# Weight conversions subtracted by TensorE in PSUM, and a head that copies the first grams' blocks first, in a kernel of attention and two expert layers

## Chip, cores and metric

The kernel runs on one core of a Trainium2 chip, in one launch. The metric is the device time of one execution in microseconds (us). TensorE (PE) multiplies matrices into PSUM; VectorE (DVE), ScalarE (ACT) and GpSimd (POOL) do the rest, each with a queue of its own that it works off in order.

## The reference

Three parts follow one another. The first is delta-rule attention over 4 batches, 8 heads, 768 tokens and 48 columns:

```python
k_n = k / (np.linalg.norm(k, axis=-1, keepdims=True) + 1e-06)
for t in range(S):
    y[:, :, t] = einsum('bhd,bhde->bhe', q[:, :, t], state)
    v_old = einsum('bhde,bhd->bhe', state, k_n[:, :, t])
    state = state + beta[:, :, t] * outer(k_n[:, :, t], v[:, :, t] - v_old)
```

The second works on its output as 3072 tokens of 384 columns: `h = x @ w_in` (384 to 2048 columns), `g = max(0.01 * h, h)`, `g @ w_out` (back to 384). The third picks one of eight experts for each token by the largest gate logit, computes `max(x @ w1[e], 0) @ w2[e]` and scales the row by the gate's probability and a sigmoid. The weights w_in and w_out come as 64-bit floats.

## The kernel before

The 768 tokens are cut into 12 chunks of 64. A chunk's attention is solved in closed form: a gram matrix of its keys (`gram`, line 104, TensorE, 48 or 64 wide tiles), its inverse by elimination (`inverse`, lines 207 to 211), and a chain of small matmuls that carries the state on (`chain`). Every operand of TensorE is two fp16 halves, high and low, and a product is three passes (high by high, high by low, low by high). The low half is the remainder: the source less the high half.

Chunks are handled in pairs w = 0 to 5. `k_load` brings the keys (kt), `k_split` makes the halves kc, `q_split` the halves q, `k_gram` multiplies and `k_gram_out` copies out of the gram's banks: the diagonal blocks go to td (eight small copies a chunk, line 131), the others as halves to lx (ScalarE the high half, line 141, VectorE the remainder, line 142). `norms` transposes td on VectorE (line 156), computes the norms and the masked matrix x; `inverse` eliminates 30 columns of x; line 211 is its last multiplication; `flipped` transposes x to zt on VectorE (line 218), and `z_make` makes the halves z of it (ScalarE line 235, VectorE line 236). For pair 0 norms and elimination run on VectorE, for all later pairs on GpSimd. The high half r in the chain (line 294, ScalarE) starts the solve.

`split_wide` (lines 71 to 79) has two forms. With wide unset ScalarE makes the scaled high half (line 78) and VectorE the remainder (line 79); with wide set ScalarE scales in place (line 74), ScalarE makes the high half (line 75) and GpSimd subtracts (line 76).

The first expert layer has its two weights converted on the chip, in 24 pieces of 128x512 (`conv`, n = 0 to 23): VectorE puts the high and the low words of the 64-bit floats together to a 32-bit one in three passes over a PSUM tile wt (lines 444 to 446), ScalarE scales it to ws in SBUF (line 451) and makes the high half (line 452), GpSimd subtracts (line 453):

```python
ws = pool.tile([128, 512], F32, tag="wt", name=f"ws_{n}")
A.activation(ws, w32, AF.Copy, scale=sc)
A.activation(h, ws, AF.Copy)
G.tensor_tensor(l, ws, h, op=ALU.subtract)
```

`weave` sets the order. Its head makes the grams, the norms and the inverse of pair 0 and the first chain. Then come 96 steps n, chunk p = n // 8, part s = n % 8. The steps of chunk 0 hold two conversions each (0 to 15), those of chunk 1 one (16 to 23). From n = 8 on each step also holds an eighth of the first expert layer for the chunk before: `moe1_up` (18 matmuls per step, tile hp; then ScalarE g, line 498, VectorE max into the bank, line 499, ScalarE gh, line 500, VectorE gl, line 501) and one step later `moe1_down` (line 512, 12 matmuls into two long-lived banks). The tiles wt and hp come from one pool psL of two banks, in turns; the odd conversions up to 7 take the banks of the downs' sums. Up to step 16 a scheduler places each engine's instructions by its own estimates; from there TensorE's order is the program's. `issue_after` blocks name an instruction behind which others have to stand. The halves of the second layer's expert weights (lines 476 and 477) start at step 16.

Of the kernel before, what the change touches and what calls it, by code (L numbers as in the profile page):

```python
# [8 lines left out]
F32 = mybir.dt.float32  # L9
F16 = mybir.dt.float16  # L10
I32 = mybir.dt.int32
AF = mybir.ActivationFunctionType
ALU = mybir.AluOpType
# [19 lines left out]
def quarter(s, h):  # L33
    return slice(64 * s + 32 * h, 64 * s + 32 * h + 32)
# [36 lines left out]
def split_wide(k, hi, lo, src, scale, wide):  # L71
    nc = k.nc
    if wide:
        nc.scalar.activation(src, src, AF.Copy, scale=scale)
        nc.scalar.activation(hi, src, AF.Copy)
        nc.gpsimd.tensor_tensor(lo, src, hi, op=ALU.subtract)
    else:
        nc.scalar.activation(hi, src, AF.Copy, scale=scale)
        nc.vector.scalar_tensor_tensor(lo, src, scale, hi, op0=ALU.mult, op1=ALU.subtract)


def k_tiles(k, c):
    t = k.chunks[c]
    t.kc, t.lx, t.z = k.kc[c % 4], k.lx[c % 4], k.z[c % 2]
    return t


def k_split(k, c, wide=False):
    t = k_tiles(k, c)
    split_wide(k, t.kc[:, 0], t.kc[:, 1], t.kt, 512.0, wide)  # L90
# [16 lines left out]
def gram_banks(k, c):  # L107
    ps, tags = (k.psO, ("psO0", "psO1")) if c in (1, 2) else (k.psS, ("psS", "psS"))
    return [ps.tile([128, GM, 64], F32, tag=tags[ab], name=f"ga{c}_{ab}") for ab in range(2)]


def k_gram(k, c, td, wide=False):
    t = k.chunks[c]
    ga = gram_banks(k, c)
    gram(k, ga, t.kc, t.kc, ALL4)
    k_gram_out(k, c, td, ga, wide)


def k_gram_out(k, c, td, ga, wide=False):
    nc = k.nc  # L120
    V, A = nc.vector, nc.scalar
    t = k.chunks[c]
    for ab in range(2):
        o = 16 * (c % 2) + GM * ab
        for s in range(2):
            for h in range(2):
                dst, src = td[quarter(s, h), :, o : o + GM], ga[ab][quarter(s, h), :, 32 * h : 32 * h + 32].rearrange("p m i -> p i m")
                if c < 2 and s:
                    k.mark_tv = V.tensor_copy(dst, src)
                else:  # L130
                    k.mark_td = A.activation(dst, src, AF.Copy)
    for ab in range(2):
        ms = slice(GM * ab, GM * ab + GM)
        src, hi, lo = ga[ab][:, :, 32 - 32 * ab : 64 - 32 * ab], t.lx[:, 0, ms], t.lx[:, 1, ms]
        if wide:
            l32 = k.m2.tile([128, GM, 32], F32, tag="gh", name=f"l32{c}_{ab}")
            A.activation(l32, src, AF.Copy, scale=2.0**-8)
            A.activation(hi, l32, AF.Copy)
            nc.gpsimd.tensor_tensor(lo, l32, hi, op=ALU.subtract)
        else:  # L140
            A.activation(hi, src, AF.Copy, scale=2.0**-8)
            V.scalar_tensor_tensor(lo, src, 2.0**-8, hi, op0=ALU.mult, op1=ALU.subtract)
# [85 lines left out]
    k.chunks[c].nw = s.nw[:, 16 * (c % 2) : 16 * (c % 2) + 16]  # L228


def z_make(k, c, s):
    nc = k.nc
    t = k.chunks[c]
    src = s.zt[:, :, 16 * (c % 2) : 16 * (c % 2) + 16].rearrange("p i m -> p m i")
    nc.scalar.activation(t.z[:, 0], src, AF.Copy)  # L235
    k.after = nc.vector.tensor_tensor(t.z[:, 1], src, t.z[:, 0], op=ALU.subtract)


def q_load(k, c):
# [6 lines left out]
def q_split(k, c, wide=False):  # L246
    t = k.chunks[c]
    t.q = k.p1.tile([112, 2, NST, 64], F16, tag="q", name=f"q{c}")
    t.ap = k.p1.tile([128, 2, NST, 64], F16, tag="ap", name=f"ap{c}")
    split_wide(k, t.q[:, 0], t.q[:, 1], t.qt, 512.0, wide)  # L250
# [143 lines left out]
def moe1_setup(k):  # L394
    nc, sb = k.nc, k.const
    V, A, G = nc.vector, nc.scalar, nc.gpsimd
    k.wg = [sb.tile([128, 3, 16], F16, name=f"wg{h}") for h in range(2)]
    wg32 = sb.tile([128, 3, 16], F32, name="wg32")
    nc.sync.dma_start(wg32, k.wg_d.rearrange("p (a e) -> p a e", a=3))
    A.activation(k.wg[0], wg32, AF.Copy, scale=1024.0)  # L400
    V.scalar_tensor_tensor(k.wg[1], wg32, 1024.0, k.wg[0], op0=ALU.mult, op1=ALU.subtract)
    k.cmat = sb.tile([128, 3, 128], F16, name="cmat")
    cst = k.m2.tile([128, 3, 128], F32, tag="g32", name="cmat32")
    nc.sync.dma_start(cst, k.cmat_d.rearrange("p (a j) -> p a j", a=3))
    V.tensor_copy(k.cmat, cst)
    k.ident, k.tri, k.ones = k.cmat[:, 0], k.cmat[:, 1], k.cmat[:, 2]
    k.crow = sb.tile([128, 32], F32, name="crow")
    nc.sync.dma_start(k.crow, k.crow_d)
    k.iota8, k.base, k.tid = k.crow[:, 0:8], k.crow[:, 8:16], k.crow[:, 16:18]
    k.run = sb.tile([128, 8], F32, name="run")  # L410
    V.tensor_copy(k.run, k.base)
    k.c2t = sb.tile([128, 128], F32, name="c2t")
    nc.sync.dma_start(k.c2t, k.c2_d)
    dum = k.m2.tile([1, XCOL], I32, tag="row", name="dum")
    G.memset(dum, 0)
    G.memset(dum[:, 385:386], BIG)
    nc.sync.dma_start(k.xd[DUM : DUM + 1, :], dum)
# [17 lines left out]
def conv(k, pool, n):  # L435
    nc = k.nc
    V, A, G = nc.vector, nc.scalar, nc.gpsimd
    i, which = n // 2, n % 2
    dst, sc = ((k.win, 1024.0), (k.wout, 2048.0))[which]
    w64 = k.w64.pop(n)  # L440
    ps, tag = (k.psO, f"psO{n // 2 % 2}") if n < 8 and n % 2 else (k.psL, "psL")
    wt = ps.tile([128, 512], I32, tag=tag, name=f"wt_{n}")
    lo, hi = w64[:, :, 0], w64[:, :, 1]
    V.tensor_scalar(wt, hi, 5, 2, op0=ALU.logical_shift_left, op1=ALU.logical_shift_right)
    V.scalar_tensor_tensor(wt, hi, -0x40000000, wt, op0=ALU.bitwise_and, op1=ALU.bitwise_or)
    V.scalar_tensor_tensor(wt, lo, 29, wt, op0=ALU.logical_shift_right, op1=ALU.bitwise_or)
    w32 = wt.bitcast(F32)
    cs = slice(512 * i, 512 * i + 512)
    h, l = (columns(d)[:, cs] for d in dst)
    ws = pool.tile([128, 512], F32, tag="wt", name=f"ws_{n}")  # L450
    A.activation(ws, w32, AF.Copy, scale=sc)
    A.activation(h, ws, AF.Copy)
    G.tensor_tensor(l, ws, h, op=ALU.subtract)


NB = 96
# [439 lines left out]
def weave(k):  # L896
    nc = k.nc
    prep_done = {}

    def prepare(w):  # L900
        a, b = 2 * w, 2 * w + 1
        wide = w == 1
        td = (k.xp if wide else k.p1).tile([128, 32, 32], F32, tag="xx" if wide else "td", name=f"td{w}")
        if not wide:
            k_split(k, a)
        yield
        if not wide:
            k_load(k, b)
        yield
        if wide:  # L910
            k_gram(k, a, td)
        else:
            k_split(k, b)
        yield
        if not wide:
            k_gram(k, a, td)
        yield
        if wide:
            k_split(k, b, True)
        else:  # L920
            k_gram(k, b, td)
        yield
        if wide:
            k_gram(k, b, td)
            yield
            yield
        with k.tc.high_priority() if w == 1 else ExitStack():
            s = norms(k, w, td)
        yield
        cuts = (1, 6, 10, 14, 18, 23, 31)  # L930
        for i in range(6):
            inverse(k, w, s, cuts[i], cuts[i + 1])
            if i == 5:
                nv_load(k, a)
            yield
        done = k.after
        with k.tc.issue_after(done.ins):
            nv_make(k, a, s)
        nv_load(k, b)
        yield  # L940
        with k.tc.issue_after(done.ins):
            nv_make(k, b, s)
        if not wide:
            yield
            yield
            yield
            yield
        with k.tc.issue_after(k.mark_gl.ins) if hasattr(k, "mark_gl") else ExitStack():
            flipped(k, w, s)
        z_make(k, a, s)  # L950
        if wide:
            yield
        z_make(k, b, s)

    def run(g):
# [15 lines left out]
    conv_load(k, wst, 1)  # L971
    nconv, nback = 0, 0
    td = k.p1.tile([128, 32, 32], F32, tag="td", name="td0")
    for c in range(2):
        k_tiles(k, c)
        ga = gram_banks(k, c)
        for s in range(2):
            k_split_half(k, c, s)
            gram(k, ga, k.chunks[c].kc, k.chunks[c].kc, ((0, s), (1, s)))
        k_gram_out(k, c, td, ga)  # L980
    mark_td = k.mark_td
    k_split(k, 2)
    q_split(k, 0)
    s0 = norms(k, 0, td)
    masked_scale(k, s0)
    nv_make(k, 0, s0)
# [40 lines left out]
    for n in range(8 * NCH):  # L1027
        p, s = n // 8, n % 8
# [6 lines left out]
        else:  # L1035
            nv_make(k, 1, s0)
        if n == 1:
            z_make(k, 1, s0)
        if n == 3:
            hold.close()  # L1040
            hold.enter_context(k.tc.issue_after(k.mark_u.ins))
# [210 lines left out]
```

## Time and profile before

| | |
|---|---|
| median of 3 runs | 920.44 us (918.71 to 921.25) |
| the profiled execution | 919.24 us, its span 917.4 us |
| mean granted clock of TensorE | 0.969 of full |
| TensorE matmuls, weight loads | 768.7 us (84%), 590.7 us (64%) |
| VectorE | 592.6 us (65%) |
| ScalarE | 405.2 us (44%) |
| GpSimd | 356.6 us (39%) |

The busy times are parts of the span, and the engines overlap; a share is a mean over stages that have different limits. A row of the timeline has the start in us from the span's start, the duration of one instruction or of a run of like ones, and in square brackets the idle time of that engine just before and what ended it. The clock of 1.00 is the higher of TensorE's two levels, 0.50 the lower.

### The profile page before, as it was taken

The page shows a single profiled execution, that of the slowest core. Times are in us where ns is not written, and L with a number is a line of the kernel's source. Part 1 is how long each engine was busy: PE and PEld are TensorE (multiplying, and loading weights), DVE is VectorE, ACT ScalarE, POOL GpSimd, SP SyncE. Part 2 cuts the span into 40 slices and gives each one's busy share as a digit, 9 for nine tenths or more (in the row PEclk, how much of TensorE's full clock was granted, in tenths as well). Part 3 has the DMA queues.
Part 4 walks back from the last instruction along what each step waited for, and adds up shares of the span by engine and source line. Part 5 has one row for each costly group of instructions (what it writes and reads, how often), then busy time and mean ns, then how long its engine had stood idle before and what let it go on. Part 6 is the DMA issues. An engine that isn't in the chain of part 4 may idle for free. (4 is left out here: it accounts for less than half of the span.)

```text
span 917.4 us, 36446 instructions
## 1 busy us (share of the span) xinstructions
PE 768.7 (84%) x15996; PEld 590.7 (64%) x15996; DVE 592.6 (65%) x1304; ACT 405.2 (44%) x788; POOL 356.6 (39%) x526
## 2 busy tenths in 40 slices
PE   3024597798979897899889899999987999999993
PEld 3023465576757665677666677777766887777782
DVE  5999985697868877788868787868445222222221
ACT  6237654655574546556665565544321111111110
POOL 0027896388118940697048800001105121222110
PEclk9999999799989998999999999999999999999997
DMA  8525432357554554556555646463934724699350
GB/s 265 176 80 156 140 127 58 86 173 182 152 143 155 165 176 143 132 172 172 168 121 167 168 128 175 122 160 120 421 144 98 218 76 150 186 311 301 104 152 12
DMA packets 100965, 145.67 MB, mean 159 GB/s; under 512 B 43120, under 2 KB 70547, under 8 KB 97986
## 3 DMA queue, kind: packets, MB, share of 16 engines
q1 hardware_dynamic: 95682, 128.29, 47.4%
q0 software_dynamic: 5120, 15.00, 5.3%
q8 instruction: 127, 2.08, 0.9%
q14 instruction: 36, 0.29, 0.1%
HBM read 152.28 MB, written 35.42 MB: 205 GB/s over the span
## 5 line engine op out<-in xcount | busy, mean ns | idle before, releaser
L493 PE MATMUL h<-xx,win 128*128 128x256 f16 x1728 | 218.6, 284 | 3.3 <-issue 1.7
L493 PEld LDWEIGHTS <-win 128*128 128x128 f16 x1728 | 169.6, 101 | 33.2 <-issue 3.6
L512 PE MATMUL o<-wout,gh 128*128 128x384 f16 x768 | 188.2, 330 | 3.2 <-DVE row L536 1.8
L512 PE MATMUL o<-wout,gl 128*128 128x384 f16 x384 | 124.4, 329 | 0.4 <-DVE gl L501 0.2
L838 PEld LDWEIGHTS <-wb 128*128 128x128 f16 x2016 | 116.5, 98 | 11.4 <-issue 7.8
L633 POOL DMA_INDIRECT xd<-row,pi x24 | 26.9, 1120 | 243.4 <-ACT gh L500 158.4
L842 DVE SCALAR_TENSOR_TENSOR h<-hp,h 128x512 f16<-128x512 f32 x48 | 33.2, 691 | 124.8 <-ACT h L841 124.8
L500 ACT ACTIVATE gh<-h 128x512 f16<-128x512 f32 x96 | 57.3, 597 | 119.2 <-DVE h L499 119.2
L838 PE MATMUL hp<-xT,wb 128*128 128x128 f16 x1728 | 101.5, 220 | 5.8 <-DMA xT<-row 5.8
L512 PEld LDWEIGHTS <-gh 128*128 128x128 f16 x768 | 73.1, 99 | 45.5 <-issue 4.5
L841 ACT ACTIVATE h<-hp 128x512 f16<-128x512 f32 x48 | 28.7, 597 | 164.9 <-PE hp L838 164.9
L852 PE MATMUL o<-wb,h 128*128 128x384 f16 x576 | 97.4, 326 | 0.0
L501 DVE TENSOR_TENSOR gl<-h,gh 128x512 f16<-128x512 f32 x96 | 66.3, 690 | 44.8 <-ACT gh L500 44.5
L209 POOL TENSOR_TENSOR x<-x,tmp 128x30 f32<-128x30 f32 (+9 forms) x150 | 90.5, 604 | 11.3
L207 POOL TENSOR_TENSOR tmp<-x 128x30 f32<-128x30 f32 (+9 forms) x150 | 86.6, 577 | 11.0
L498 ACT ACTIVATE g<-h 128x512 f32<-128x512 f32 x96 | 57.5, 599 | 63.7 <-PE h L493 58.8
L499 DVE SCALAR_TENSOR_TENSOR h<-h,g 128x512 f32<-128x512 f32 x96 | 66.4, 691 | 29.5 <-ACT g L498 29.0
L856 POOL DMA_INDIRECT out_dram<-y,row x24 | 23.9, 998 | 147.0 <-DVE y L855 125.5
L852 PEld LDWEIGHTS <-h 128*128 128x128 f16 x576 | 55.4, 98 | 34.3
L477 DVE SCALAR_TENSOR_TENSOR whl<-we,whl 128x512 f16<-128x512 f32 x96 | 72.6, 768 | 0.0
L302 PE MATMUL ks<-r,z 32*32 32x48 f16 x2304 | 27.7, 188 | 46.7 <-ACT z L235 27.1
L476 ACT ACTIVATE whl<-we 128x512 f16<-128x512 f32 x96 | 57.9, 622 | 0.0
(250 smaller groups left out, 1131.4 us busy)
## 6 DMA issues: line engine op xcount, KB each, us to landing
wb<-wd SPq DMA_DIRECT2D x56, 1536.0 KB
we<-in_we_dram SPq DMA_DIRECT2D x96, 256.0 KB
wd<-whl SPq DMA_DIRECT2D x96, 256.0 KB
kt<-in_kt_dram SPq DMA_DIRECT2D x22, 224.0 KB
qt<-in_qt_dram SPq DMA_DIRECT2D x22, 224.0 KB
nv<-in_kv_dram SPq DMA_DIRECT2D x12, 384.0 KB
kn<-in_kv_dram SPq DMA_DIRECT2D x12, 384.0 KB
w<-in_win_dram SPq DMA_DIRECT2D x6, 512.0 KB
```

The costliest lines, as they stand in the source:

```text
L207: E.tensor_tensor(tv, x[:, q, j : j + 1].to_broadcast([128, n, j]), x[:, j : j + 1, 0:j].to_broadcast([128, n, j]), op=ALU.mult)
L209: k.after = E.tensor_tensor(x[:, q, 0:j], x[:, q, 0:j], tv, op=ALU.add)
L476: nc.scalar.activation(hl[:, 0], w32, AF.Copy, scale=sc)
L477: nc.vector.scalar_tensor_tensor(hl[:, 1], w32, sc, hl[:, 0], op0=ALU.mult, op1=ALU.subtract)
L493: PE.matmul(hp[:, ff], k.win[l][:, f, kk], xx[:, r, kk], start=(n == 0), stop=(n == 8))
L498: A.activation(g32, hp, AF.Copy, scale=0.01 * 2.0**-10)
L499: V.scalar_tensor_tensor(hp, hp, 2.0**-10, g32, op0=ALU.mult, op1=ALU.max)
L500: k.mark = A.activation(gh, hp, AF.Copy)
L501: k.mark_gl = V.tensor_tensor(gl, hp, gh, op=ALU.subtract)
L512: k.mark_down = k.nc.tensor.matmul(k.o[t], gg[l][:, ff, 128 * t : 128 * t + 128], k.wout[r][:, f], start=(f == 0 and i == 0), stop=(f == N ...
L838: PE.matmul(hp[:, ff], w1[:, l, kk, 128 * f : 128 * f + 128], t.xT[:, 3 * r + kk], start=(i == 0), stop=(i == 8))
L852: nc.tensor.matmul(o, t.h[l][:, f], w2[:, r, f], start=(i == 0), stop=(i == 23))
```

## The change

It has three parts.

1. In `conv` TensorE first writes two products of the identity into the wt bank (128x384 and 128x128), then VectorE's three passes overwrite it as before; ScalarE makes the scaled high half straight from the bank, TensorE adds `minus` times the high half to the bank (a diagonal of -2^-10 or -2^-11), which leaves the unscaled remainder there, and ScalarE copies the remainder, scaled, to the low half. The tile ws and GpSimd's subtraction are gone. The bank stays taken until the low half is copied.
2. `k_gram_out` is cut in two. For chunks 0 and 1 all copies to td come first; behind them, and behind VectorE's last td copy, the others (`k_lx_out`) in their wide form, with the remainder on GpSimd.
3. `k_split` of chunk 2 and `q_split` of chunk 0 in the head, and `k_gram` of chunk 2, take the wide form; the second `z_make` (chunk 1) has its remainder on GpSimd.

```diff
-def k_gram_out(k, c, td, ga, wide=False):
+    k_td_out(k, c, td, ga)
+    k_lx_out(k, c, ga, wide)
+def k_td_out(k, c, td, ga):
...
+def k_lx_out(k, c, ga, wide=False):
...
-def z_make(k, c, s):
+def z_make(k, c, s, E=None):
...
-    k.after = nc.vector.tensor_tensor(t.z[:, 1], src, t.z[:, 0], op=ALU.subtract)
+    k.after = (E or nc.vector).tensor_tensor(t.z[:, 1], src, t.z[:, 0], op=ALU.subtract)
...
+    k.minus = sb.tile([128, 2, 128], F16, name="minus")
+    for w, x in enumerate((-(2.0**-10), -(2.0**-11))):
+        G.tensor_scalar(k.minus[:, w], k.ident, x, None, op0=ALU.mult)
...
+    nc.tensor.matmul(wt.bitcast(F32)[:, 0:384], k.ident, k.cmat.rearrange("p a j -> p (a j)"), start=True, stop=True)
+    nc.tensor.matmul(wt.bitcast(F32)[:, 384:512], k.ident, k.ident, start=False, stop=True, skip_group_check=True)
     V.tensor_scalar(wt, hi, 5, 2, op0=ALU.logical_shift_left, op1=ALU.logical_shift_right)
...
-    ws = pool.tile([128, 512], F32, tag="wt", name=f"ws_{n}")
-    A.activation(ws, w32, AF.Copy, scale=sc)
-    A.activation(h, ws, AF.Copy)
-    G.tensor_tensor(l, ws, h, op=ALU.subtract)
+    A.activation(h, w32, AF.Copy, scale=sc)
+    nc.tensor.matmul(w32, k.minus[:, which], h, start=False, stop=True, skip_group_check=True)
+    A.activation(l, w32, AF.Copy, scale=sc)
...
-            k_gram(k, a, td)
+            k_gram(k, a, td, True)
...
-        k_gram_out(k, c, td, ga)
+        k_td_out(k, c, td, ga)
+        gas.append(ga)
...
-    k_split(k, 2)
-    q_split(k, 0)
+    with k.tc.issue_after(mark_td.ins), k.tc.issue_after(k.mark_tv.ins):
+        for c in range(2):
+            k_lx_out(k, c, gas[c], True)
+        k_split(k, 2, True)
+        q_split(k, 0, True)
...
-            z_make(k, 1, s0)
+            z_make(k, 1, s0, nc.gpsimd)
```

Line numbers below 117 are the same in the changed kernel, later ones are 9 to 18 higher: conv's passes are lines 458 to 460, its copies 464 and 466, its matmuls 456, 457 and 465; g is 511, max 512, gh 513, gl 514, the downs 525.

GpSimd's queue at the head, up to the copy named turn, which stands behind the first z. Before:

```order
L191 AFFINE_SELECT zm<-zm 128x1024
L994 CAST turn<-z_114 128x1
L76 TENSOR_TENSOR kc_109<-kt_555,kc_109 112x1024
L76 TENSOR_TENSOR kg_788<-kn_558,kg_788 128x768
L453 TENSOR_TENSOR win_94<-ws_938,win_93 128x512
```

Now:

```order
L418 TENSOR_SCALAR minus<-cmat 128x128 x2
L148 TENSOR_TENSOR lx_110<-l_0_355,lx_110 128x256
L148 TENSOR_TENSOR lx_110<-l_1_359,lx_110 128x256
L76 TENSOR_TENSOR kc_108<-wout_96,kc_108 112x1024
L76 TENSOR_TENSOR q_374<-wout_95,q_374 112x1024
L148 TENSOR_TENSOR lx_111<-l_0_363,lx_111 128x256
L148 TENSOR_TENSOR lx_111<-l_1_367,lx_111 128x256
L200 AFFINE_SELECT zm<-zm 128x1024
L1012 CAST turn<-z_114 128x1
```

The keys of chunk 2 (kc_108) and the queries of chunk 0 (q_374) lie staged in the tiles of wout. Six remainders stand on GpSimd ahead of the mask zm that were VectorE's.

ScalarE's queue in the steps of chunk 1 that hold conversions 21 and 22 (wt_2732 and wt_2787 before, wt_2770 and wt_2826 now) and parts 5 and 6 of chunk 0's first layer. Before:

```order
L498 ACTIVATE g_5_2761<-h_5_2742 128x512
L451 ACTIVATE ws_2791<-wt_2787 128x512
L500 ACTIVATE gh_5_2762<-h_5_2742 128x512
L452 ACTIVATE win_93<-ws_2791 128x512
L498 ACTIVATE g_6_2814<-h_6_2795 128x512
```

Now:

```order
L464 ACTIVATE wout_95<-wt_2770 128x512
L511 ACTIVATE g_5_2800<-h_5_2781 128x512
L466 ACTIVATE wout_96<-wt_2770 128x512
L513 ACTIVATE gh_5_2801<-h_5_2781 128x512
L464 ACTIVATE win_93<-wt_2826 128x512
L511 ACTIVATE g_6_2854<-h_6_2835 128x512
L513 ACTIVATE gh_6_2855<-h_6_2835 128x512
L466 ACTIVATE win_94<-wt_2826 128x512
```

The copy of the low half out of the bank (line 466) stands one or two activations behind that of the high half, and both read the bank. TensorE's queue at the same place, now:

```order
L525 MATMUL o_2086<-wout_95,gh_4_2640 128x384
L465 LDWEIGHTS minus
L465 MATMUL wt_2770<-wout_95,minus 128x512
L525 LDWEIGHTS gh_4_2640
L525 MATMUL o_2086<-wout_96,gh_4_2640 128x384
L525 LDWEIGHTS gl_4_2641
L525 MATMUL o_2086<-wout_95,gl_4_2641 128x384
L456 LDWEIGHTS cmat
L456 MATMUL wt_2826<-cmat 128x384
L457 LDWEIGHTS cmat
L457 MATMUL wt_2826<-cmat 128x128
L525 LDWEIGHTS gh_5_2801
```

The subtraction for conversion 21 and the identities for conversion 22 stand among the downs, two downs apart; neither was there before.

VectorE's queue around the transposition of pair 1 (zt). Before:

```order
L499 SCALAR_TENSOR_TENSOR h_7_2953<-h_7_2953,g_7_2972 128x512
L501 TENSOR_TENSOR gl_7_2974<-h_7_2953,gh_7_2973 128x512
L218 STREAM_TRANSPOSE zt_2217<-x_902 128x1024
L236 TENSOR_TENSOR z_114<-zt_2217,z_114 128x512
L236 TENSOR_TENSOR z_115<-zt_2217,z_115 128x512
```

Now:

```order
L512 SCALAR_TENSOR_TENSOR h_2_2212<-h_2_2212,g_2_2231 128x512
L460 SCALAR_TENSOR_TENSOR wt_2201<-w_18_1897,wt_2201 128x512
L514 TENSOR_TENSOR gl_2_2233<-h_2_2212,gh_2_2232 128x512
L227 STREAM_TRANSPOSE zt_2253<-x_919 128x1024
L326 SCALAR_TENSOR_TENSOR ks_3023<-nv_1942,nw_924 128x384
```

It stood behind the eighth part of chunk 0's first layer (h_7) and stands behind the third now (h_2), with passes of conversions 19 to 23 behind it.

## Rows read from the trace of the kernel before

**Rows 1.** Windows: us; busy us of PE, PEld, DVE, ACT, POOL; PEclk; DMA share; GB/s

```profile
30.00:40.00 10.00, 0.00 (x0) 0.00 (x0) 10.00 (x54) 3.03 (x9) 0.83 (x1) 1.00 0.44 113
...
120.00:130.00 10.00, 10.00 (x165) 7.28 (x164) 8.51 (x15) 6.67 (x12) 9.29 (x14) 1.00 0.45 157
150.00:160.00 10.00, 5.08 (x150) 3.88 (x137) 3.44 (x4) 3.72 (x7) 4.45 (x8) 0.86 0.31 82
...
158.00:160.00 2.00, 0.00 (x0) 0.00 (x0) 1.30 (x2) 1.95 (x6) 0.00 (x0) 0.50 0.00 0
```

**Rows 2.** Timeline, 113 to 170 us: start, us, engine, line, what; [idle before <-releaser]

```profile
150.97 2.14 PE L493 MATMUL h<-xx,win 128*128 128x256 f16 x18
...
162.12 1.82 PE L104 MATMUL ga<-kc 48*64 48x64 f16 x96 [7.04 <-DVE lx L142]
166.15 4.02 PE L493 MATMUL h<-xx,win 128*128 128x256 f16 x18
...
154.96 1.25 DVE L218 STREAM_TRANSPOSE zt<-x 128x1024 f32<-128x1024 f32 x1 [4.73 <-POOL x L211]
...
113.51 0.59 ACT L498 ACTIVATE g<-h 128x512 f32<-128x512 f32 x1
...
147.54 0.60 ACT L498 ACTIVATE g<-h 128x512 f32<-128x512 f32 x1 [1.00 <-PE h L493]
...
156.24 2.01 ACT L235 ACTIVATE z<-zt 128x512 f16<-128x512 f32 x2 [6.73 <-DVE zt L218]
158.16 3.06 ACT L131 ACTIVATE td<-ga 32x256 f32<-32x256 f32 x8
...
163.46 0.62 ACT L498 ACTIVATE g<-h 128x512 f32<-128x512 f32 x1
```

**Rows 3.** GpSimd: timeline at 76 and 153 us; by line: busy us, mean ns, idle before

```profile
76.41 0.24 POOL L164 TENSOR_TENSOR nz<-ny 128x32 f32<-128x32 f32 x1 [3.01 <-DVE ny L162]
...
153.01 1.91 POOL L211 TENSOR_TENSOR x<-x,nz 128x1024 f32<-128x1024 f32 x1
...
L453 POOL TENSOR_TENSOR win<-ws,win 128x512 f16<-128x512 f32 x12 | 14.3, 1190 | 12.0 <-ACT win L452 11.9
```

**Rows 4.** Timeline of the head, 18 to 29 us, VectorE and ScalarE

```profile
20.40 0.42 DVE L142 SCALAR_TENSOR_TENSOR lx<-ga,lx 128x256 f16<-128x256 f32 x1 [0.24 <-ACT lx L141]
...
28.54 0.28 DVE L209 TENSOR_TENSOR x<-x,tmp 128x14 f32<-128x14 f32 x2
...
18.17 1.06 ACT L74 ACTIVATE kt<-kt 112x1024 f32<-112x1024 f32 x1 [0.56 <-DMA kt<-in_kt_dram]
...
25.53 0.96 ACT L294 ACTIVATE r<-ks 128x384 f16<-128x384 f32 x2 [3.22 <-DVE ks L317]
```

**Rows 5.** Timeline of GpSimd, 53 us: a remainder of 112x1024

```profile
53.63 2.13 POOL L76 TENSOR_TENSOR kc<-kt,kc 112x1024 f16<-112x1024 f32 x1
```

**Rows 6.** Timeline, 29 and 77 us: VectorE beside GpSimd

```profile
29.44 1.43 DVE L209 TENSOR_TENSOR x<-x,tmp 128x36 f32<-128x36 f32 x2
...
29.55 1.28 POOL L191 TENSOR_SCALAR_AFFINE_SELECT zm<-zm 128x1024 f32<-128x1024 f32 x1 [28.18 <-ACT zm L190]
...
76.85 2.03 DVE L79 SCALAR_TENSOR_TENSOR kc<-kt,kc 112x1024 f16<-112x1024 f32 x1
...
76.64 1.15 POOL L453 TENSOR_TENSOR wout<-ws,wout 128x512 f16<-128x512 f32 x1
```

**Rows 7.** Timeline, 56 to 110 us, VectorE and ScalarE

```profile
56.38 1.78 DVE L236 TENSOR_TENSOR z<-zt,z 128x512 f16<-128x512 f32 x1
...
109.33 0.68 DVE L446 SCALAR_TENSOR_TENSOR wt<-w,wt 128x512 int32<-128x512 int32 x1
...
67.92 3.06 ACT L131 ACTIVATE td<-ga 32x256 f32<-32x256 f32 x8
```

**Rows 8.** Timeline of TensorE, 144 us: downs of one part

```profile
144.04 0.49 PE L512 MATMUL o<-wout,gh 128*128 128x384 f16 x2
144.37 0.33 PE L512 MATMUL o<-wout,gl 128*128 128x384 f16 x1
```

More of the change, by code (lines that the diff above doesn't have):

```diff
@@ L119, in k_gram_out @@
 def k_gram_out(k, c, td, ga, wide=False):
-    nc = k.nc
-    V, A = nc.vector, nc.scalar
-    t = k.chunks[c]
+    k_td_out(k, c, td, ga)
+    k_lx_out(k, c, ga, wide)
+def k_td_out(k, c, td, ga):
+    V, A = k.nc.vector, k.nc.scalar
     for ab in range(2):
@@ L131, in k_gram_out @@
                     k.mark_td = A.activation(dst, src, AF.Copy)
+def k_lx_out(k, c, ga, wide=False):
+    nc = k.nc
+    V, A = nc.vector, nc.scalar
+    t = k.chunks[c]
     for ab in range(2):
@@ L973, in weave @@
     td = k.p1.tile([128, 32, 32], F32, tag="td", name="td0")
+    gas = []
     for c in range(2):
```

## The prediction

> **What bounds the kernel now.** I read the part by engine and the forty slices first: TensorE is busy for 84% of the span, but its row of digits has thin places at the start and in one slice near 160 us, so a change that touches the first 170 us is judged there and not by the average. The table of windows shows the same in numbers [rows 1]: from 30 to 40 us VectorE alone is busy without a gap (the elimination of the first pair of chunks), from 120 to 130 us TensorE has no gap and the three others are busy for 67 to 93%, and from 150 to 160 us none is busy for over 51%. That last hole I followed through the timeline of each engine [rows 2]: VectorE's transposition waits 4.73 us for GpSimd's last multiplication, ScalarE's copy of z waits 6.73 us for the transposition, eight td copies of 3.06 us follow, TensorE's gram waits 7.04 us, and the first activation of the next chunk comes 15.9 us after the last one (147.54 to 163.46), where eight ones stood 4.86 us apart (113.51 to 147.54 is seven steps) [rows 2]. In the hole the granted clock goes down to 0.50 [rows 1], the lower of its two levels, and the eighteen up matmuls that take 2.14 us at 150.97 take 4.02 at 166.15 [rows 2]. GpSimd is late because its queue holds the norms and the elimination of the second pair and, between them, the subtractions of the converted weights, twelve for each of the two weights, at 1.19 us [rows 3]. Behind the steps of chunk 0 the change alters no instruction, so I let a shift at that point stand to the end.
>
> All sums are against the profiled execution, 919.24 us, which is 1.2 us under the median of the runs shown (920.44). A difference of 0.3%, 2.8 us, is about what a measurement of this kernel tells from none.
>
> **Head, 18 to 49 us.** Two remainders leave VectorE (0.42 us each [rows 4]), and they go in front of its wait for ScalarE, so they gain nothing on the path. Between the td copies and r ScalarE gets eight copies more: four of 112x1024, near 1.06 us as the scaling copy of kt [rows 4], and four of 128x256, taken at half of the 0.60 us of a 128x512 activation [rows 2]: 4.2 + 1.2 = 5.4 us. ScalarE idled 3.22 us there [rows 4], so r comes 2.2 us later. GpSimd gets four remainders of a quarter of 2.13 us and two of 2.13 us [rows 5], 6.4 us in all, and they fall at about 24 to 33 us, into VectorE's first columns. What that costs is bounded by pairs of rows: VectorE's pair of additions took 1.43 us while GpSimd selected for 1.28 us, where the pair before took 0.28; its remainder of kc took 2.03 us starting 0.21 us behind a GpSimd subtraction of 1.15 us [rows 4, 6]. So a two-input operation of VectorE seems to wait for the rest of GpSimd's instruction. The lower bound is nothing (all of it beside VectorE's wait for r), the upper the whole 6.4 us. I take 2.9 us: the two wide ones less the 1.4 us or so in which VectorE still waits for r. The head costs 2.2 + 2.9 = **+5.1 us**.
>
> The Trainium skill (SBUF — State Buffer, section Who interferes with whom) states that a VectorE instruction with two SBUF inputs contends with a GpSimd instruction that reads SBUF, and that the loser is blocked fully, for the whole instruction. Taken to the letter the whole 6.4 us would be added here and the sum would end 3.5 us higher, an estimate by that page; the rows agree on the mechanism, and where the work falls decides the size.
>
> **52 to 112 us.** VectorE loses the second z remainder (1.78 us [rows 7]) and two remainders of chunk 2, 0.8 by the row of the head: -2.6 us. Two new waits stand in the queues: ScalarE's r of the first chain now stands behind four copies out of the banks, of which two, 1.2 us, lie beyond its wait, and VectorE's transposition of the second pair waits for r and for eight td copies (3.06 us [rows 7]) of which 2.4 us are not covered: +3.6 us. GpSimd's own subtractions no longer press on VectorE, which I leave at zero with a gain of up to 1 us. At the first g of chunk 0 one copy of a conversion (0.60) and one subtraction of TensorE stand ahead that did not: +1.0 us. So the first g comes at +5.1 - 2.6 + 3.6 + 1.0 = **+7.1 us**, near 120.6 instead of 113.51 [rows 2].
>
> The conversions themselves fall back further than that, since each now holds its bank through h copy, subtraction and l copy. The third pass of conversion 16 (109.33, 0.68 us [rows 7]) I find at about 119; it feeds the next part.
>
> **Steps of chunk 0, 113 to 148 us.** The wt tile and the hp tile take turns in two banks, one conversion and one h tile per step, so each of the two goes round in one bank of its own. Before, the hp bank set the step: ups 2.14, g 0.60, max, gh 0.60, gl, with about 0.68 us for each of VectorE's [rows 2, 7], 4.7 us of the 4.86. Now the wt bank goes round through three engines. A matmul of 512 columns is worked out from the downs: two of 384 columns stand 0.33 us apart [rows 8], 0.165 each by throughput, 0.22 for 512 columns, and 0.33 from start to end, near 0.43 for 512. The round is h copy 0.60, subtraction 0.43, l copy 0.60, identities 0.43, three passes 3 x 0.68 = 2.04: 4.1 us. In the order printed above g stands between the two copies on ScalarE (0.60 less the 0.43 beside which it runs, 0.2), max and gl stand among the passes on VectorE (1.4), and two to six downs stand ahead of each of the two TensorE parts (0.3 to 1.0 each way): 6.0 to 7.0 us. I take 6.4, since the downs ahead of the subtraction mostly run while g does: 7 x (6.4 - 4.86) = **+10.8 us**. The lower bound is TensorE's own time alone, 2 x 0.22 = 0.44 us for each of eight conversions in a stretch where it has no gap [rows 1]: +3.5 us. The upper is 7.0 us a step: +15 us.
>
> **The hole, 148 to 163 us.** Of the 24 subtractions three stood ahead of GpSimd's norms (76.41 [rows 3]) and twenty-one behind, 21 x 1.15 = 24 us; without them its last multiplication ends at about 130 instead of 154.9 (153.01 + 1.91 [rows 3]). In the order printed above VectorE's transposition now stands behind the third gl of chunk 0, no longer behind the eighth; it comes to it near 120.6 + 2 x 6.4 + 1.6 = 135 and waits for nothing. The z copies and the gram move into the steps above (z 2.0 and r 1.0 us of ScalarE are in the 6.4), the last g and the next first g are one more step apart: 6.4 instead of 15.9, **-9.5 us**, the half clock gone with it.
>
> **Sum:** 7.1 + 10.8 - 9.5 = +8.4, 919.24 + 8.4 = 927.6, said as **928 us**; its own range is 923 to 935. GpSimd's two small multiplications that make the constant stand before 20 us, where it idled until 29.55 [rows 6]: nothing.
>
> **Rivals.**
> *Faster: the hole goes and the banks do not bind.* If VectorE's and ScalarE's new instructions fit into their gaps (15 and 33% in [rows 1]), the steps grow by TensorE's time alone, +3.5, and GpSimd's early remainders meet VectorE's wait: head +1.0, then -2.6, the hole -9.5, together -7.6: 911.6 us. For it: all three engines had some idle time in the steps, and the hole is the largest loss that the trace shows before 170 us. Against it: the round through three engines is longer than the step of before by itself once max and gl are counted. It decides at about 5.6 us a step: below that the hole outweighs the steps and the head. Chance 0.30.
> *About the same.* The head costs what I say (+6.1 at 112 us), the steps grow by TensorE's time alone, the hole goes: 6.1 + 3.5 - 9.5 = +0.1, 919.3 us. Chance 0.12.
> *The hole stays.* The change does not do what the trace would let it do: if GpSimd is blocked by VectorE's passes and additions as VectorE is by it, or the norms start over 5 us later than I find (130 against 135 us), the transposition waits again. The head and the steps are then paid and nothing comes back: 937 us with a full hole, 932 with half of it. Chance 0.08.
>
> **How the numbers follow.** The forecast has 0.50: head, steps and hole each as above. Slower by over 0.3% is the forecast but for a sliver, and the last rival: 0.56. Faster by over 0.3% is the first rival and the edge of the second: 0.32. The rest is 0.12. The range goes from 909 (the first rival with a head that costs nothing, 910.6, and VectorE's 1 us) to 935 (the forecast with 7.0 us a step is 932, and the head's upper bound adds 3.5); it leaves out the full hole and the low end of the first rival.
>
> **What the profile after would show.** Right: ScalarE's r near 28 us and VectorE's first pairs of additions lengthened beside GpSimd's 112x1024 remainders; the first g near 120 us; eight g about 6.4 us apart; the transposition of the second pair without a wait for GpSimd, GpSimd done near 130 us; no half clock near 165 us. Wrong: g 5 to 5.3 us apart (then the banks do not bind, and the time is under 920), a first g before 116 us (the head was hidden), or a transposition that still waits for GpSimd's multiplication.

## The result and the profile after

The changed kernel took 930.36 us (median of 6 runs, 927.21 to 933.75) and the kernel before 919.02 (6 runs, 916.27 to 921.25): a ratio of 1.0126, 95% interval 1.0096 to 1.0155, 11 us slower. Six more executions, beside the last experiments, came to 1.0114 (1.0078 to 1.0150). The forecast was 928, within 909 to 935. The profiled execution of the changed kernel took 929.99 us, its span is 928.3, 10.9 us more than before. The part by engine of its page (busy us, share of the span, instructions):

```profile
PE 792.7 (85%) x16068; PEld 598.7 (64%) x16068; DVE 590.3 (64%) x1295; ACT 407.7 (44%) x796; POOL 337.2 (36%) x513
```

GpSimd lost 19.4 us, VectorE 2.3; TensorE is busy for 24 us more, with 72 matmuls more. None of this says where the time went; that is read from the timeline.

**Head.** VectorE, GpSimd and ScalarE of the changed kernel (start, us, engine, line):

```profile
24.04 2.04 DVE L182 TENSOR_SCALAR ny<-ny 128x32 f32<-128x32 f32 x1
...
26.50 1.67 DVE L184 TENSOR_TENSOR nz<-nz 128x32 f32<-128x32 f32 x1
...
53.83 1.25 DVE L227 STREAM_TRANSPOSE zt<-x 128x1024 f32<-128x1024 f32 x1
...
23.91 2.13 POOL L76 TENSOR_TENSOR kc<-wout,kc 112x1024 f16<-112x1024 f32 x1
26.00 2.12 POOL L76 TENSOR_TENSOR q<-wout,q 112x1024 f16<-112x1024 f32 x1
...
28.68 0.96 ACT L303 ACTIVATE r<-ks 128x384 f16<-128x384 f32 x2 [1.69 <-DVE ks L326]
```

and of the kernel before, the same two operations of VectorE and its first transposition to z:

```profile
24.20 0.18 DVE L173 TENSOR_SCALAR ny<-ny 128x32 f32<-128x32 f32 x1
...
24.80 0.19 DVE L175 TENSOR_TENSOR nz<-nz 128x32 f32<-128x32 f32 x1
...
50.02 1.25 DVE L218 STREAM_TRANSPOSE zt<-x 128x1024 f32<-128x1024 f32 x1
```

Two operations on 32 columns take 2.04 and 1.67 us instead of 0.18 and 0.19. Each ends 0.04 to 0.05 us after the GpSimd subtraction beside which it started (26.08 and 26.04; 28.17 and 28.12). ScalarE was ready: it waits 1.69 us for VectorE. At the transposition the head is 3.8 us late, 3.3 of them from these two operations. The first of the two has a single input in SBUF, so the hold is wider than the two-input operations that the prediction named. The Trainium skill (SBUF — State Buffer, section Who interferes with whom) has a sentence on that, too: a tensor_scalar may run in a mode that takes the shared ports, and the other engine then blocks fully; the first row agrees. The second operation reads SBUF twice and falls under the sentence that the prediction named.

**First layer of chunk 0.** ScalarE, VectorE, GpSimd and TensorE of the changed kernel:

```profile
118.84 0.60 ACT L466 ACTIVATE wout<-wt 128x512 f16<-128x512 f32 x1 [0.42 <-PE wt L465]
...
123.95 0.60 ACT L511 ACTIVATE g<-h 128x512 f32<-128x512 f32 x1 [1.09 <-PE h L506]
...
172.43 0.60 ACT L511 ACTIVATE g<-h 128x512 f32<-128x512 f32 x1 [2.67 <-PE h L506]
...
178.67 0.60 ACT L511 ACTIVATE g<-h 128x512 f32<-128x512 f32 x1
...
137.94 1.23 DVE L227 STREAM_TRANSPOSE zt<-x 128x1024 f32<-128x1024 f32 x1
...
141.79 1.96 DVE L245 TENSOR_TENSOR z<-zt,z 128x512 f16<-128x512 f32 x2
...
126.99 1.91 POOL L220 TENSOR_TENSOR x<-x,nz 128x1024 f32<-128x1024 f32 x1
...
119.89 4.02 PE L506 MATMUL h<-xx,win 128*128 128x256 f16 x18
...
157.07 4.02 PE L506 MATMUL h<-xx,win 128*128 128x256 f16 x18 [0.82 <-DVE gl L514]
```

Against [rows 2]: the first g comes at 123.95 instead of 113.51 (+10.4). The last is 48.48 us behind it instead of 34.03, 6.93 us a step (+14.5). The first g of the next chunk follows 6.24 us later instead of 15.92 (-9.7): GpSimd is done at 128.9 instead of 154.9, VectorE's transposition waits for nothing. There the shift is +15.2 us: 10.4 of it stand ahead of the first g, and the steps and the hole together add 4.8. At the end it is +10.9: 4.3 us come back later.

The first h tile's ups (119.89) start 0.45 us after ScalarE has copied the low half of conversion 15 out of the bank (118.84 + 0.60). The seven steps are not alike: 5.51, 5.59, 6.92, 9.41, 9.81, 6.12, 5.12 us. (Those of the kernel before were not either: 2.32 to 6.87.) The two long ones hold z (1.96 us of VectorE), kc and r of the next chunks, which stood in the hole before. The slow ups come up twice (4.02 us for 2.14). At 157.07 TensorE had stood idle, and the windows show the lower level, at 119.89 the higher:

```profile
158.00:160.00 2.00, 2.00 (x11) 1.41 (x10) 0.00 (x0) 0.58 (x1) 0.00 (x0) 0.50 0.70 217
...
118.00:124.00 6.00, 6.00 (x69) 3.50 (x63) 2.45 (x4) 2.16 (x5) 5.14 (x12) 1.00 0.12 33
```

Why the ups at 119.89 stretch the profile does not say. The change did not bring it: the first ups of the kernel before are as slow, also at 1.00:

```profile
109.09 3.97 PE L493 MATMUL h<-xx,win 128*128 128x256 f16 x18 [0.74 <-ACT ws L451]
...
109.00:113.00 4.00, 3.91 (x20) 2.55 (x19) 3.65 (x6) 2.28 (x5) 3.77 (x7) 1.00 0.39 131
```

### The profile page after: what moved, and what is told of

Read it like the earlier page. It is cut to its first block, busy times and chain, and to the rows that moved or that the text cites. A ratio compares the mean times of both kernels' runs of the same rounds, so it can differ in the third digit from the quotient of the medians.

```text
span 928.3 us, 36579 instructions
## 1 busy us (share of the span) xinstructions
PE 792.7 (85%) x16068; PEld 598.7 (64%) x16068; DVE 590.3 (64%) x1295; ACT 407.7 (44%) x796; POOL 337.2 (36%) x513
## 5 line engine op out<-in xcount | busy, mean ns | idle before, releaser
L506 PE MATMUL h<-xx,win 128*128 128x256 f16 x1728 | 221.8, 286 | 4.7 <-issue 3.3
L851 PEld LDWEIGHTS <-wb 128*128 128x128 f16 x2016 | 116.8, 99 | 10.8 <-issue 4.5
L218 POOL TENSOR_TENSOR x<-x,tmp 128x30 f32<-128x30 f32 (+9 forms) x150 | 92.3, 615 | 11.8
L311 PE MATMUL ks<-r,z 32*32 32x48 f16 x2304 | 27.8, 188 | 33.0 <-ACT z L244 19.4
```

The source lines that it names most:

```text
L218: k.after = E.tensor_tensor(x[:, q, 0:j], x[:, q, 0:j], tv, op=ALU.add)
L506: PE.matmul(hp[:, ff], k.win[l][:, f, kk], xx[:, r, kk], start=(n == 0), stop=(n == 8))
L851: PE.matmul(hp[:, ff], w1[:, l, kk, 128 * f : 128 * f + 128], t.xT[:, 3 * r + kk], start=(i == 0), stop=(i == 8))
```

## The experiments

The theory was the sum of the prediction: GpSimd's remainders hold the head up, banks held through three engines make the conversions' work late and long, the hole pays part of it back. All ratios are to the kernel before on the same chip, with their 95% intervals; the times expected stand against some 919 us for it, and it took 923.57 (median) beside the first four runs, so the ratios decide.

**The two parts apart.** The first run takes the changed kernel and puts conv back, the second puts the head back:

```diff
-    A.activation(h, w32, AF.Copy, scale=sc)
-    nc.tensor.matmul(w32, k.minus[:, which], h, start=False, stop=True, skip_group_check=True)
-    A.activation(l, w32, AF.Copy, scale=sc)
+    ws = pool.tile([128, 512], F32, tag="wt", name=f"ws_{n}")
+    A.activation(ws, w32, AF.Copy, scale=sc)
+    A.activation(h, ws, AF.Copy)
+    G.tensor_tensor(l, ws, h, op=ALU.subtract)
```

> The head's part of the change alone: the copies of the first grams' blocks first, early remainders and the second z remainder on GpSimd; the conversions as before. Theory (the sum of the prediction): VectorE's norms are held up by GpSimd's 112x1024 remainders, the transposition of pair 0 starts near 53.8 us instead of 50.0, the hole before the second chunk of the first layer stays, since GpSimd still has the 24 subtractions: 921 to 925 us. Rival (all of the loss is in the conversions): 918 to 920.5 us, the transposition of pair 0 whenever it likes, its delay taken up by waits further on.

> The conversions' part of the change alone, the head as before. Theory: the transposition of pair 0 is back near 50 us, the hole is gone (no wait of VectorE's transposition of pair 1 for GpSimd), the eight g of chunk 0 stand 6 to 7 us apart, the first g some 4 us earlier than in the changed kernel: 924 to 928 us. Rival (the head is the whole loss, the conversions pay for themselves): under 920 us.

The head alone: 1.0011 (0.9977 to 1.0045). The conversions alone: 1.0121 (1.0076 to 1.0166), the whole loss, some 930 us against 919 and more than was expected. The timeline of the head alone:

```profile
53.52 1.25 DVE L227 STREAM_TRANSPOSE zt<-x 128x1024 f32<-128x1024 f32 x1
...
156.35 1.25 DVE L227 STREAM_TRANSPOSE zt<-x 128x1024 f32<-128x1024 f32 x1 [4.38 <-POOL x L220]
...
114.73 0.59 ACT L507 ACTIVATE g<-h 128x512 f32<-128x512 f32 x1
```

The transposition is 3.5 us late, as expected, the first g only 1.2: waits further on take the delay up, and the time stays below what was expected of it. That is the rival's side of that run, though the interval reaches into both ranges; the hole stays, as expected. In the run of the conversions alone the hole is gone and the steps take 6.76 us, as expected, but the first g is later than in the changed kernel, not earlier:

```profile
126.12 0.60 ACT L511 ACTIVATE g<-h 128x512 f32<-128x512 f32 x1 [1.75 <-PE h L506]
```

So the late first g is the conversions' doing. The two parts do not add there: +1.2 and +12.6 us apart, +10.4 together.

**The head's remainders back on VectorE** (`k_split(k, 2)` and `q_split(k, 0)` without the wide form):

> The changed kernel with the two early 112x1024 remainders (keys of chunk 2, queries of chunk 0) back on VectorE and their scaling copies gone from ScalarE; the four 128x256 ones stay on GpSimd. Theory: VectorE's 128x32 operations of the norms are back at 0.19 us (2.04 and 1.67 in the changed kernel), it pays two remainders of about 1.2 us, and the transposition of pair 0 starts at 51 to 52.5: 926.5 to 929.5 us. Rival (ScalarE's longer queue holds the head up, not GpSimd): 128x32 operations as long as in the changed kernel, or the same start: 930 us.

```profile
20.26 1.18 DVE L79 SCALAR_TENSOR_TENSOR kc<-wout,kc 112x1024 f16<-112x1024 f32 x1
21.46 1.22 DVE L79 SCALAR_TENSOR_TENSOR q<-wout,q 112x1024 f16<-112x1024 f32 x1
...
27.00 0.18 DVE L182 TENSOR_SCALAR ny<-ny 128x32 f32<-128x32 f32 x1
...
52.87 1.25 DVE L227 STREAM_TRANSPOSE zt<-x 128x1024 f32<-128x1024 f32 x1
```

The 0.18 us are back, which shows that the 112x1024 remainders did the holding. But VectorE pays 2.4 us for them itself: the transposition gains 1.0 us (52.87, expected 51 to 52.5), the first g (123.86) nothing. The ratio of 1.0104 (1.0054 to 1.0153) is not told apart from the changed kernel's.

**Conversions 16 to 23 as before**, the others the new way (`old = n >= 16` ahead of the two forms):

> The changed kernel with conversions 16 to 23, those in the steps of chunk 0's first layer, done as before (ScalarE to SBUF, GpSimd subtracts, bank free after one copy). Theory (the bank's round sets the steps): the eight g stand 4.9 to 5.6 us apart instead of 6.9, GpSimd's last multiplication ends near 138 us, still at VectorE's transposition, so no hole: 919 to 924 us. Rival (TensorE's own added time is the loss): a third of the added matmuls goes, 3.5 us: 926 to 927.5 us. Rival (the work moved out of the hole fills the steps, not the bank): steps stay at 6.4 or more, 927 to 931 us.

```profile
124.39 0.59 ACT L519 ACTIVATE g<-h 128x512 f32<-128x512 f32 x1
...
160.56 0.60 ACT L519 ACTIVATE g<-h 128x512 f32<-128x512 f32 x1 [0.51 <-PE h L514]
167.07 0.60 ACT L519 ACTIVATE g<-h 128x512 f32<-128x512 f32 x1
```

Steps of 5.17 us instead of 6.93, and 0.9966 (0.9937 to 0.9995), better than expected: the whole loss is gone, some 15 us by the ratios, 11.6 of them by the first g of chunk 1 (167.07 against 178.67). TensorE's own added time does not reach that far: a third of it was expected to be 3.5 us, and a third of the 24 us that its busy time grew by is 8. GpSimd is done at 130.2, not near 138. One step of 9.73 us is left, with z in it.

**Its counterpart, conversions 0 to 15 as before** (`old = n < 16`):

> The changed kernel with conversions 0 to 15 done as before and only 16 to 23 the new way (the counterpart of the run with 16 to 23 as before). Theory (banks held through three engines set both the late first g and the long steps): the first g comes at 114 to 117 us instead of 124, the steps stay at 6 us or more, and GpSimd, with sixteen subtractions back in its queue, ends near 145 us, after VectorE has come to its transposition (behind the third gl, near 130), so VectorE waits there for over 8 us: ratio to the kernel before 1.008 to 1.02. Rival (the first g is late because of the head): first g still later than 121 us.

```profile
114.11 0.60 ACT L519 ACTIVATE g<-h 128x512 f32<-128x512 f32 x1 [2.04 <-PE h L514]
...
149.03 1.25 DVE L227 STREAM_TRANSPOSE zt<-x 128x1024 f32<-128x1024 f32 x1 [4.77 <-POOL x L220]
```

The first g is back at 114, GpSimd ends at 149.0, 4 us later than expected, and VectorE waits for it 4.77 us, not over 8, in the middle of chunk 0: one step takes 13.87 us, the mean is 7.68. The ratio is 1.0010 (0.9980 to 1.0040), better than expected.

**More banks, nothing else**:

```diff
-    ps, tag = (k.psO, f"psO{n // 2 % 2}") if n < 8 and n % 2 else (k.psL, "psL")
+    ps, tag = (k.psO, f"psO{n // 2 % 2}") if n < 16 and n % 2 else (k.psL, "psL")
```

> The changed kernel with the odd conversions up to 15, not only up to 7, in the banks of the downs' sums, which are free until the second part of chunk 0: four banks for the conversions instead of two, nothing else changed. Theory (the first h tile waits for the bank of conversion 15): the first g 3 to 7 us earlier, at 117 to 121 us, steps still 6.5 to 7 us, ratio to the kernel before 1.003 to 1.010 (the changed kernel 1.0126). Rival (the passes and copies of VectorE and ScalarE themselves, or TensorE's half clock, set the late start): first g at 123 to 125 us, ratio 1.011 to 1.014.

```profile
112.93 3.31 PE L506 MATMUL h<-xx,win 128*128 128x256 f16 x16
...
116.99 0.59 ACT L511 ACTIVATE g<-h 128x512 f32<-128x512 f32 x1
...
160.77 0.60 ACT L511 ACTIVATE g<-h 128x512 f32<-128x512 f32 x1 [0.97 <-PE h L506]
```

0.9980 (0.9952 to 1.0007), more than was expected, with every copy, subtraction and identity of the changed kernel still there. The first ups start 7.0 us earlier, the steps fall to 6.25, and the first g of chunk 1 comes at 168.00, 10.7 us earlier than in the changed kernel and 4.5 later than in the kernel before. So waiting for banks is most of the 15.2 us: 10.7 go with the added work untouched. What keeps the steps at 6.25, where conversions 16 to 23 still share two banks with the h tiles, is not told apart: the banks, the added work and z, kc and r all stand there. And that the ratio comes down to 0.998 is not the banks' doing alone; some 5 us come back behind chunk 0 (below).

**Both reliefs, and versions with fewer new conversions**, made of the edits above:

> Both reliefs together: odd conversions up to 15 in the banks of the downs' sums, conversions 16 to 23 as before. If the two effects add: first g at 117 to 121 us, steps near 5.2 us, no hole (GpSimd ends near 138 us, the transposition stands behind the third gl; a wait of up to 4 us there if the first g comes at 117), ratio to the kernel before 0.990 to 0.996. If the late start is no matter of banks: as the run with 16 to 23 as before, 0.9966.

> The kernel before with only conversions 0 to 7, which have four banks, done the new way; the head as before. GpSimd loses eight subtractions, 9.5 us, and ends near 146 us; the transposition of pair 1 now stands behind the fourth gl of chunk 0. Theory: first g at 113 to 116 us, steps 4.9 to 5.3, with a wait of VectorE for GpSimd of 5 to 12 us in the middle of chunk 0 in place of the hole: ratio 0.992 to 1.002. Rival (the new conversions cost by themselves, wherever they stand): first g later than 118 us, ratio over 1.005.

> A version that may beat both: the head of the kernel before, conversions 0 to 11 the new way, 12 to 23 as before, odd ones up to 15 in the banks of the downs' sums. Theory: GpSimd with twelve subtractions less ends near 135 us, at VectorE's transposition (behind the third gl, near 132), so the wait of the run with 0 to 7 the new way (2.44 us) is gone or stays under 3 us; first g at 114 to 118 us, steps near 5.5 us: ratio to the kernel before 0.990 to 0.996. Rival (what the hole gives is eaten by the steps wherever the subtractions go): 0.996 to 1.000.

> Conversions 0 to 15 the new way, 16 to 23 as before, odd ones up to 15 in the banks of the downs' sums, and the head of the kernel before (its counterpart with the changed head ran at 0.9976). If the head's 3 to 4 us at the transposition of pair 0 reach the end once the conversions no longer bind: 0.992 to 0.995. If they are taken up on the way, as in the run of the head alone: 0.996 to 0.999.

In that order they came to 0.9976 (0.9953 to 0.9999), 0.9964 (0.9939 to 0.9989), 1.0030 (1.0004 to 1.0055), outside of both that were expected, and 0.9973 (0.9947 to 0.9999), the side on which the head's delay is taken up on the way. The reliefs do not add. With both of them the first g is at 117.44 and VectorE's transposition waits 1.61 us for GpSimd, but the steps take 5.65 us; z, kc and r, I take it, have to be done somewhere. From the first g of chunk 0 to that of chunk 1 it is 48.3 us, where the kernel before needed 50.0. The lowest ratio is that of eight new conversions in four banks with the head of before, 0.4% under the kernel before, though it is not told apart from the others below 1. Its parts were not as expected: the first g comes at 119.13, which was the rival's sign, the steps take 5.78 us, and VectorE's wait is shorter (the row of both reliefs first, then two of this run):

```profile
131.28 1.25 DVE L227 STREAM_TRANSPOSE zt<-x 128x1024 f32<-128x1024 f32 x1 [1.61 <-POOL x L220]
...
119.13 0.60 ACT L519 ACTIVATE g<-h 128x512 f32<-128x512 f32 x1 [1.65 <-PE h L514]
...
141.10 1.25 DVE L227 STREAM_TRANSPOSE zt<-x 128x1024 f32<-128x1024 f32 x1 [2.44 <-POOL x L220]
```

Why eight new conversions, with four banks and the head of before, delay the first g by 5.6 us and sixteen do not (113.76) stays open. The rows of g, against those of the kernel before (us), tell where each version gains:

| | first g of chunk 0 | first g of chunk 1 | last g of the first layer | ratio |
|---|---|---|---|---|
| the changed kernel | +10.4 | +15.2 | +12.0 | 1.0126 |
| more banks, nothing else | +3.5 | +4.5 | -0.3 | 0.9980 |
| both reliefs | +3.9 | +2.3 | -1.2 | 0.9976 |
| eight new, head of before | +5.6 | +2.5 | -5.7 | 0.9964 |
| twelve new, head of before | +5.0 | +3.7 | -0.7 | 1.0030 |
| sixteen new, head of before | +0.2 | +0.7 | -4.1 | 0.9973 |

The second trace of the kernel before stays within 0.2 us of the first at all three places. No version is ahead when chunk 1 begins; what puts some under the kernel before comes behind, where no instruction is altered. Why twelve (1.0030) are worse than eight or sixteen was not found: GpSimd ends at 134.7, the transposition does not wait, and the steps take 5.61 us; most of the difference to eight arises behind chunk 0.

**Where 4.3 us came back.** Both kernels once more, for their traces:

> The changed kernel once more, on the chip of the other three runs. Ratio to the kernel before 1.009 to 1.016. In the trace: first g at 124, first g of the next chunk near 179 us. If TensorE's pauses for nothing that the profile shows (third to fourth part of a chunk) belong to the kernel, the same chunks have steps over 7 us there as in the first trace (chunks 2, 5, 6, 9 and 10); if they are chance, others.

> The kernel before once more, for its trace alone. If the pauses belong to the kernel: steps over 7 us from the third to the fourth part in chunks 1 to 5 and 7 to 9, and some 6 us more of them in all than in the changed kernel; if they are chance: other chunks and a sum that may come out either way.

The second trace of the changed kernel has its first g at 124.50 and that of the next chunk at 181.10, 2 us later than expected, with steps of 7.19 us. In the chunks without a pause g follows g by 6.4 us from the third part to the fourth; in the others, all but chunk 5 of the kernel before, TensorE pauses there for nothing that the profile shows (it says issue), and in some it then runs at the lower level. In the kernel before (chunk 2; two rows of TensorE's timeline, then the window behind):

```profile
227.79 0.53 PE L302 MATMUL ks<-r,z 32*32 32x48 f16 x48 [1.61 <-issue]
228.25 3.38 PE L493 MATMUL h<-xx,win 128*128 128x256 f16 x18
...
230.00:232.00 2.00, 2.00 (x10) 1.29 (x9) 0.00 (x0) 0.28 (x1) 1.35 (x2) 0.50 0.34 123
```

In the changed kernel (chunk 10):

```profile
622.12 0.22 PE L311 MATMUL ks<-r,z 32*32 32x48 f16 x6 [2.12 <-issue]
622.27 3.81 PE L506 MATMUL h<-xx,win 128*128 128x256 f16 x18
```

The step is longer than 7 us in chunks 1 to 5 and 7 to 9 of the kernel before, in both traces (7.0 for the ninth of the second one), and in 2, 5, 6, 9 and 10 of the changed one, in both, with 8 at 7.1 in the second. So the pauses belong to the program. Over chunks 1 to 10 these steps take 17.4 and 19.7 us more than 6.4 each before, and 11.8 and 11.7 after: 5.6 and 8.0 less. All other steps up to the last g of the first layer take 2.4 us more, so 3.2 and 5.6 us come back there; the account goes by the steps, and pauses stand in other steps too.

The traces tell more of these pauses. Count TensorE's matmuls and weight loads in the order in which they start: in all fourteen traces, each of the 120 pauses over 0.6 us between 150 and 670 us that the profile puts down to issue stands ahead of an instruction whose count is 193 over a multiple of 256. And each ends 1.2 to 1.7 us after a transfer of 16384 bytes on the queue that the page of the kernel before lists so (packets, MB, share):

```profile
q8 instruction: 127, 2.08, 0.9%
```

That is one such transfer for some 252 of the 32060 matmuls and weight loads recorded. In chunk 2 above the last 256 of them began at 224.33 us, the transfer ran from 224.72 to 226.38, and TensorE went on at 227.79. So it seems to wait there for its next block of instructions, where it has worked off the block before too quickly; at some nine of ten such places it does not pause. The change puts 144 instructions more (72 matmuls, 72 weight loads) ahead of chunk 1, which moves the places against the program. No run varies this alone, so it is read from the traces and not shown by an experiment.

## Why the prediction was right

The direction held, and of the cause the main part: banks held longer cost more than the hole gives back. +8.4 us was forecast against the profiled execution, +10.8 was measured there (929.99 against 919.24). That the size is so near is partly luck: the head was counted too high, the conversions ahead of the first g too low, and 4.3 us came back that no term foresaw.

- **The hole**: -9.5 forecast, -9.7 measured. GpSimd's end (130, measured 128.9), the place of the transposition (135, measured 137.9) and the missing wait came as worked out.
- **The steps**: 6.4 us each forecast, 6.93 measured (7.19 in the second trace), at the upper end of 6.0 to 7.0 or past it; +14.5 us for +10.8. The parts were not right: four of the seven steps take 5.1 to 6.1 us, below the 6.4 that I took, and the two that take z, kc and r take over 9. I had counted that work into the 6.4. Nor do the terms give that range: 4.1 + 0.2 + 1.4 and two waits of 0.3 to 1.0 are 6.3 to 7.7. The mean is near by errors that cancel.
- **The head**: the failed term. I had ScalarE's longer queue delay r by 2.2 us and the shared ports add 2.9. ScalarE idled 1.69 us ahead of r, so its queue cost nothing; VectorE's held-up operations make 3.3 of the 3.8 us at the transposition, and by the run of the head alone 1.2 are left at the first g and 0.1% of the time.
- **52 to 112 us**: the term "At the first g of chunk 0", +1.0 us, was mis-sized. I saw the conversions fall back (the third pass of conversion 16 near 119; it came at 121.6), but let only the steps pay. The first h tile needs the bank of conversion 15, and with the conversions alone changed the first g is 12.6 us late. The errors of head and conversions partly cancel: +7.1 forecast, +10.4 measured.
- **"The half clock gone with it"** was wrong: the lower level comes back at 158 us.
- **Behind chunk 0** I let the shift stand, as no instruction is altered there; it shrank by 4.3 us, 3.2 of them in the steps of the first layer, where the pauses above moved.
- The rival "the banks do not bind" had the right condition. Given two more banks the kernel is where "about the same" puts it, but not by its terms: the first g is 3.5 us late, not 6.1, and the steps cost 9.7 us, not 3.5.

## What to carry to other kernels

An engine relieved of work is not the gain; ask what is now held for longer. Here a PSUM bank that was free after one copy waited for a copy, a matmul and a second copy on three queues, and two more banks took away 10.7 of the 15.2 us without touching the work. Where versions differ by a few tenths of a percent, see at which point of the program the time is gained: here it was gained where nothing had been changed. Before a subtraction leaves an idle engine, count the rounds of the buffer that it would keep busy.

## What was not expected of the hardware

A VectorE operation on 32 columns with one SBUF input lasted 2.04 us instead of 0.18 while GpSimd subtracted beside it, to within 0.05 us of that instruction's end. TensorE pauses of 0.7 to 4.2 us in the two kernels, put down to nothing by the profile, come at places that lie multiples of 256 TensorE instructions apart, 1.2 to 1.7 us after a transfer of 16384 bytes on the queue named instruction; the eighteen ups behind some of them take 3.2 to 3.8 us instead of 2.1, where the granted clock fell (0.50 in the window shown).
